# Converted weights are stored some pulls of the background queue later, and the words of the conversion lie in PSUM during the expert stage

## The chip, the core and the metric

The kernel runs on one core of a Trainium2 chip: TensorE (PE) with its weight loads (PEld), VectorE (DVE), ScalarE (ACT), GpSimd (POOL) and SyncE (SP), which issues nearly all DMA transfers. The metric is the device time of one execution in microseconds (us), as the median of several runs.

## What is computed

Three layers follow one another on 3072 tokens of width 384. The second is a top-1 mixture of 8 experts, and the third a gated product of two projections.

```python
# 1. gated linear attention (per batch and head)
state = f * state + k (outer) v ;  y = q @ state
# 2. mixture of experts: each token goes to one of 8 experts
h = maximum(x[mask] @ w1[e], 0);  out[mask] = gate * (h @ w2[e])
# 3. a, b = x @ w1, x @ w2;  out = ((a * b) @ w3) @ w_out
```

The weights of the third layer (w1, w2, w3, w_out of `moe2`) come as 64-bit floats. The kernel turns them into 32-bit floats by integer and scaling operations on the two 32-bit words of each number.

## The kernel before

The work is in three stages: attention with routing (to about 177 us of the profiled execution), the expert stage (about 177 to 424 us), and the gated layer (to the end). The order of instructions on each engine is written out by hand; engines run independently and wait for each other by semaphores.

**Expert stage.** Experts are taken one after another, `for e in range(E)`, with a window of 448 down to 376 tokens each. Each expert has eight steps `s`, one per 128 hidden units. In a step PE computes `hb` (`g1_step`, nine matmuls), then `acc` of the step before (`g2_step(e, s - 1)`, nine matmuls), so hidden units are used one step after they are made. Between the two, ACT makes `h[0] = relu(hb)` (L1030) and DVE the remainder `h[1]` (L1031); `acc` reads both. After step 7 the next expert's tokens are transposed (`xb`, L1015).

**Weights of the experts.** They are fetched by SP in halves of 768 KB into two buffers `stg` (L317): after step 3 and after step 7 the half of w1 (128x3x512), after steps 4 and 0 the half of w2 (128x4x384). ACT casts each piece (`wh`, L142) and POOL makes the remainder (`wl`, L143); these run piece by piece from a queue, `wsplit`, after each step. At step 0 SP also stores token numbers (`idd`, L995) and fetches the next expert's tokens (`xs`, L987, 675.5 KB). The gate factors are multiplied into `xs` by ACT in steps 3 to 6 (L1006).

**The background queue.** `bg` is a queue of Python generators that convert the third layer's weights; `bg.pull(n)` advances it by n places (3 per step, 4 in one expert). A piece of 128x512 numbers is converted in six pulls by `conversions`. SP loads it (`raw`, 512 KB, three buffers, L208). ACT makes the scaled low and high words (L224, L225, "the words" below). One pull later DVE shifts and masks (L227, L228). One pull later POOL adds (L230) into the tile `gt`. For the twelve pieces of w1 and w2, `to_scratch` then stores `gt` (256 KB) to a scratch tensor in device memory, `gd` (L149, "the store"). `gt` has two buffers, so the words of a piece reuse the tile of the piece two before it, and ACT waits at L224 until that tile's store has landed. The remaining eight pieces, of w3 (tile `g3`), are used in place by PE (`w3_turn`, `w3_times`).

The words of a piece stand at an odd step (1, 3, 5 or 7), behind that step's `h`; so one piece takes two steps. The loop puts the SP work of a step after its pulls:

```python
issue()
bg.pull(4 if e == E - 3 else 3)
wsplit.pull(...)
if s % 4 == 3:
    ahead = prefetch(2 * e + s // 4 + 2)
if s % 4 in (0, 3):
    step(ahead)
```

Matmul results of the expert stage lie in PSUM, in two sets of banks: three for `acc`, and five that `hb`, `xb` and the w3 tiles take in turn by `bank`. A class `Early` converts other pieces in the attention stage; there the scaled high word already lies in PSUM (`z`, L267; its bit operations are L272 and L273).

Of the kernel before, what the change touches and what calls it, by code (L numbers as in the profile page):

```python
# [10 lines left out]
I32 = mybir.dt.int32  # L11
AF = mybir.ActivationFunctionType
ALU = mybir.AluOpType
# [6 lines left out]
def attn_moe_glu_kernel(  # L20
# [17 lines left out]
    PE, V, A, G, SP = nc.tensor, nc.vector, nc.scalar, nc.gpsimd, nc.sync  # L38
# [3 lines left out]
    P = 128  # L42
# [18 lines left out]
    def bank(shape, name, tag="ps"):  # L61
        acc = tag == "acc"
        return psum[acc].tile(shape, F32, tag="acc" if acc else "ps", name=name)
# [49 lines left out]
    def f32(t):  # L113
        return t.bitcast(F32)
# [6 lines left out]
    class Background:  # L121
        def __init__(self):
            self.q = []

        def add(self, gen):
            self.q.append(gen)

        def pull(self, n):
            while n > 0 and self.q:
                try:  # L130
                    next(self.q[0])
                    n -= 1
                except StopIteration:
                    self.q.pop(0)

        def drain(self):
            while self.q:
                issue()
                self.pull(1)

    def split(src, hi, lo, eng=G):
        A.copy(out=hi, in_=src)  # L142
        eng.tensor_tensor(out=lo, in0=src, in1=f32(hi), op=ALU.subtract)  # L143

    def to_scratch(dst):
        def put(t):
            yield
            yield
            SP.dma_start(out=dst, in_=t)  # L149

        return put

# [41 lines left out]
    def issue():  # L194
        while loads:
            loads.pop(0)()

    def conversions(pieces):
        raws = {}

        def load_raw(i):
            if i < len(pieces):
                loads.append(lambda: fetch_raw(i))

        def fetch_raw(i):
            src, n, _, _ = pieces[i]
            raws[i] = cv.tile([P, 512, 2], I32, name="raw", bufs=RAW)[:, 0:n, :]
            SP.dma_start(out=raws[i], in_=src.bitcast(I32).rearrange("p (n w) -> p n w", w=2))  # L208

        for i in range(RAW):  # L210
            load_raw(i)
        for i, (_, n, tag, put) in enumerate(pieces):
            while i not in raws:
                yield
            if i == 0:
                for _ in range(8):
                    yield
            raw = raws.pop(i)
            lo, hi = raw[:, :, 0], raw[:, :, 1]
            z = lo  # L220
            pool, bufs = (cvw[1], cvw[2]) if tag == "g3" else (cv, 2)
            t = pool.tile([P, 512], F32, name=tag, bufs=bufs)[:, 0:n]
            p = t.bitcast(I32)
            A.activation(out=p, in_=lo.bitcast(U32), func=AF.Copy, scale=2.0 ** -29)  # L224
            A.activation(out=f32(z), in_=f32(hi), func=AF.Copy, scale=2.0 ** -112)  # L225
            yield
            V.tensor_scalar(out=z, in0=z, scalar1=3, scalar2=None, op0=ALU.logical_shift_left)  # L227
            V.scalar_tensor_tensor(out=z, in0=hi, scalar=-(1 << 31), in1=z, op0=ALU.bitwise_and, op1=ALU.bitwise_or)  # L228
            yield
            G.tensor_tensor(out=p, in0=z, in1=p, op=ALU.add)  # L230
            load_raw(i + RAW)
            yield
            yield
            yield from put(t)
# [58 lines left out]
    def late():  # L293
        pieces = []
        for n, g in enumerate((g1, g2)):
            for kk in range(KD):
                for c in range(FF // 512):
                    r, cs = slice(kk * P, (kk + 1) * P), slice(c * 512, (c + 1) * 512)
                    pieces.append((g[r, cs], 512, "gt", to_scratch(gd[n][r, cs])))
        return conversions(pieces + [w3_piece(i, c) for i in range(GAP_TILES, KF) for c in range(2)])  # L300
# [508 lines left out]
    with tc.manual_schedule():  # L809
# [57 lines left out]
        bg = Background()  # L867
# [379 lines left out]
        for n in range(NS):  # L1247
            end = n == NS - 1
            o1 = [bank2(1 - n % 2, DM, "ob") for _ in range(NT)]
            for s in range(KF):  # L1250
# [5 lines left out]
                if n == 0 and s == 3:  # L1256
                    t = stage[0].tile([P, KD, 512], F32R, tag="stg", name="stg")
# [164 lines left out]
```

## Time and profile before

| | us |
|---|---|
| median of 3 runs | 717.91 (717.73 to 719.16) |
| the profiled execution, its own time | 718.84 |
| its span, first to last instruction | 717.1 |
| PE busy | 698.7 (97%) |
| DVE busy | 454.4 (63%) |
| ACT busy | 364.1 (51%) |
| POOL busy | 345.1 (48%) |

The profiled execution is one run, taken by the hardware profiler; about 1.7 us of its time lie outside the span. Rows of a view give start, duration, engine, line of the kernel, operation, tiles as output<-inputs, and in square brackets the idle time just before with what ended it.

### The profile page before, as it was taken

To read this page: it belongs to the slowest core of one execution; us is meant where nothing else is said; L and a number is where in the kernel's file an instruction comes from. 1 tells how busy PE (TensorE), PEld (TensorE's weight loads), DVE (VectorE), ACT (ScalarE), POOL (GpSimd) and SP (SyncE) were. 2 spreads that over 40 slices of the span, in tenths; PEclk is the share of its full clock that TensorE was granted. 3 is DMA by queue.
4 is the path that set the end of the run, shared out by engine and by line. 5 is a ranking of instruction groups with operands and counts; after the bars stand their busy time and mean duration, and the time that the engine had idled before them with its cause. 6 is when DMAs were issued, how large, how long until landed. Compare 5 with 4: busy or idle time off the path is not lost.

```text
span 717.1 us, 13516 instructions
## 1 busy us (share of the span) xinstructions
PE 698.7 (97%) x5098; PEld 641.6 (89%) x5098; DVE 454.4 (63%) x860; ACT 364.1 (51%) x757; POOL 345.1 (48%) x420
## 2 busy tenths in 40 slices
PE   7999999999999999999999999999999999999995
PEld 6999989879999899999999998888988889888895
DVE  8989999987354554444465878854844457554461
ACT  5697877855656485555465544322522225321240
POOL 5466787784976677564660013222242222522233
PEclk9999999999999999999999999999999999999999
DMA  8999999852867758656342431000110001100002
GB/s 177 204 221 202 233 240 226 213 178 73 268 209 247 225 182 255 198 161 192 118 125 94 132 99 33 1 0 1 45 44 1 1 1 41 48 1 0 1 12 81
DMA packets 132033, 85.74 MB, mean 120 GB/s; under 512 B 106481, under 2 KB 114681, under 8 KB 131961
## 3 DMA queue, kind: packets, MB, share of 16 engines
q1 hardware_dynamic: 128489, 74.55, 38.9%
q0 software_dynamic: 3072, 9.46, 3.5%
q8 instruction: 42, 0.69, 0.4%
q10 hardware_dynamic: 400, 0.79, 0.4%
q14 instruction: 30, 0.25, 0.1%
HBM read 70.57 MB, written 14.22 MB: 118 GB/s over the span
## 4 chain that ended last, share of the span: by engine, by line
PE 63%; DMA 5%; POOL 2%; issue 2%; ACT 2%; SPq 1%; DVE 1%; POOLq 0%; DVEq 0%; ACTq 0%
PE ob L1231 14%; PE acc L1042 10%; PE hb L1028 9%; PE pd L1195 7%; PE pb L1195 7%; PE pa L1195 7%; PE pc L1195 5%; DMA stg<-in_moe_w_dram 4%; PE wpb L185 3%; POOL wl L143 1%; DMA gd<-gt 1%; PE xb L1015 1%; ACT wh L142 1%; POOL gt L230 1%; PE w3b L174 0%
## 5 line engine op out<-in xcount | busy, mean ns | idle before, releaser
L1198 POOL TENSOR_TENSOR xT<-xT,xT 128x512 f32<-128x512 f32 x48 | 63.9, 1332 | 194.0 <-ACT xT L1205 192.2
L143 POOL TENSOR_TENSOR wl<-stg,wh 128x384 fp32r<-128x384 f32 (+1 forms) x86 | 98.9, 1181 | 34.6 <-ACT wh L142 34.5
L1042 PE MATMUL acc<-h,wh 128*128 128x448 f32 (+7 forms) x384 | 105.4, 352 | 1.8 <-DVE h L1031 1.1
L1028 PE MATMUL hb<-xT,wh 128*128 128x448 f32 (+7 forms) x384 | 102.2, 347 | 0.0
L1031 DVE SCALAR_TENSOR_TENSOR h<-hb,h 128x448 fp32r<-128x448 f32 (+7 forms) x64 | 37.0, 578 | 86.5 <-ACT h L1030 86.3
L1220 ACT CAST abh<-xT 128x512 fp32r<-128x512 f32 x24 | 14.9, 621 | 133.7 <-DVE xT L1198 133.7
L1198 DVE TENSOR_TENSOR xT<-xT,pb 128x512 f32<-128x512 f32 x24 | 16.5, 688 | 97.8 <-PE pb L1195 91.4
L1042 PEld LDWEIGHTS acc<-h,wh 128*128 128x128 f32 x384 | 70.3, 188 | 6.4 <-DVE h L1031 3.6
L142 ACT CAST wh<-stg 128x384 fp32r<-128x384 f32 (+1 forms) x121 | 61.2, 562 | 25.8 <-DMA stg<-in_moe_w_dram 25.8
L1028 PEld LDWEIGHTS hb<-xT,wh 128*128 128x128 f32 x384 | 70.9, 188 | 1.2
L1028 PE MATMUL hb<-xT,wl 128*128 128x448 f32 (+7 forms) x192 | 66.6, 347 | 0.0
L1042 PE MATMUL acc<-h,wl 128*128 128x448 f32 (+7 forms) x192 | 66.6, 347 | 0.0
L1030 ACT ACTIVATE h<-hb 128x448 fp32r<-128x448 f32 (+7 forms) x64 | 32.4, 507 | 58.3 <-PE hb L1028 58.2
L1231 PE MATMUL ob<-wp,abh 128*128 128x384 f32 x240 | 61.8, 338 | 0.0
L1238 POOL DMA_INDIRECT out_dram<-h,didx x24 | 24.8, 1033 | 54.1 <-ACT h L1237 35.2
L1231 PEld LDWEIGHTS ob<-wp,abh 128*128 128x128 f32 x240 | 44.0, 188 | 1.8
L552 POOL TENSOR_SCALAR_AFFINE_SELECT am<-am 128x512 f32<-128x512 f32 x48 | 29.5, 640 | 25.8 <-ACT am L551 25.8
L1231 PE MATMUL ob<-wp,abl 128*128 128x384 f32 x120 | 40.5, 338 | 0.0
L185 PE MATMUL wpb<-wo,w3t 128*128 128x384 f32 x192 | 37.1, 341 | 0.0
L1198 DVE TENSOR_TENSOR xT<-xT,pc 128x512 f32<-128x512 f32 x48 | 33.0, 687 | 5.8 <-PE pc L1195 5.6
L1028 PEld LDWEIGHTS hb<-xT,wl 128*128 128x128 f32 x192 | 36.1, 188 | 0.6
L1042 PEld LDWEIGHTS acc<-h,wl 128*128 128x128 f32 x192 | 36.1, 188 | 0.6
(356 smaller groups left out, 1777.6 us busy)
## 6 DMA issues: line engine op xcount, KB each, us to landing
stg<-in_moe_w_dram SPq DMA_DIRECT2D x30, 768.0 KB
raw<-in_moe_w_dram SPq DMA_DIRECT2D x28, 512.0 KB
xs<-xsd SPq DMA_DIRECT2D x8, 675.5 KB
q<-in_q_dram SPq DMA_DIRECT2D x24, 192.0 KB
k<-in_k_dram SPq DMA_DIRECT2D x24, 192.0 KB
v<-in_v_dram SPq DMA_DIRECT2D x24, 192.0 KB
f<-in_f_logit_dram SPq DMA_DIRECT2D x23, 192.0 KB
raw<-in_moe_w_out_dram SPq DMA_DIRECT2D x8, 384.0 KB
```

The costliest lines, as they stand in the source:

```text
L142: A.copy(out=hi, in_=src)
L143: eng.tensor_tensor(out=lo, in0=src, in1=f32(hi), op=ALU.subtract)
L185: PE.matmul(out=o, lhsT=t[:, x, j, :], rhs=wo[:, y, j, :], start=(j + n == 0), stop=(j == KF - 1 and n == 2))
L552: G.affine_select(out=m[:, hb], in_=m[:, hb], pattern=[[0, NP], [1, P]], compare_op=ALU.is_ge, fill=0.0, base=0, channel_multiplier=-1)
L1028: PE.matmul(out=b, lhsT=w[x][:, kk, cs], rhs=xT[e][y][:, kk, :], start=(kk + n == 0), stop=(kk == KD - 1 and n == 2))
L1030: A.activation(out=h[0], in_=b, func=AF.Relu)
L1031: V.scalar_tensor_tensor(out=h[1], in0=b, scalar=0.0, in1=f32(h[0]), op0=ALU.max, op1=ALU.subtract)
L1042: PE.matmul(out=acc[d], lhsT=w[x][:, s % 4, d * P:(d + 1) * P], rhs=hs[s][y], start=(s + n == 0), stop=(s == KF - 1 and n == 2))
L1195: PE.matmul(out=o, lhsT=w[a][i][:, cs], rhs=x[b][j], start=(first and m == 0), stop=(last and m == 2), skip_group_check=True)
L1198: eng.tensor_tensor(out=out, in0=a, in1=b, op=op)
L1231: PE.matmul(out=o[t], lhsT=ab[x][:, t * P:(t + 1) * P], rhs=wp[:, y, s, :], start=(s + m == 0), stop=(s == KF - 1 and m == 2), skip_group_ ...
L1238: ins = G.indirect_dma_start(out=out, out_offset=bass.IndirectOffsetOnAxis(ap=didx[:, j:j + 1], axis=0), in_=r, in_offset=None,)
```

## The change

Two things are changed. First, `to_scratch` no longer issues the store at once. It puts it on a list, `late`, with a count of 4. `Background.tick` runs after every pull, the one of the entry too, and issues the store when its count is 0: three pulls, one step, later. Second, in `conversions` the scaled high word `z` goes to a PSUM bank of the five, in place of the `lo` half of `raw` in SBUF. DVE then takes both of its inputs' bits from `z` (the sign too, which it took from `hi` before) and writes into `lo`.

```diff
     class Background:
         def __init__(self):
             self.q = []
+            self.late = []
...
                     next(self.q[0])
                     n -= 1
+                    self.tick()
                 except StopIteration:
                     self.q.pop(0)
+
+        def tick(self):
+
+            for x in list(self.late):
+                x[0] -= 1
+                if x[0] == 0:
+                    self.late.remove(x)
+                    x[1]()
 
         def drain(self):
             while self.q:
                 issue()
                 self.pull(1)
+            while self.late:
+                self.tick()
...
             yield
             yield
-            SP.dma_start(out=dst, in_=t)
+            bg.late.append([4, lambda: SP.dma_start(out=dst, in_=t)])
...
             lo, hi = raw[:, :, 0], raw[:, :, 1]
-            z = lo
+            z = bank([P, 512], "z")[:, 0:n]
...
             A.activation(out=p, in_=lo.bitcast(U32), func=AF.Copy, scale=2.0 ** -29)
-            A.activation(out=f32(z), in_=f32(hi), func=AF.Copy, scale=2.0 ** -112)
-            yield
-            V.tensor_scalar(out=z, in0=z, scalar1=3, scalar2=None, op0=ALU.logical_shift_left)
-            V.scalar_tensor_tensor(out=z, in0=hi, scalar=-(1 << 31), in1=z, op0=ALU.bitwise_and, op1=ALU.bitwise_or)
-            yield
-            G.tensor_tensor(out=p, in0=z, in1=p, op=ALU.add)
+            A.activation(out=z, in_=f32(hi), func=AF.Copy, scale=2.0 ** -112)
+            yield
+            z = z.bitcast(I32)
+            V.tensor_scalar(out=lo, in0=z, scalar1=3, scalar2=None, op0=ALU.logical_shift_left)
+            V.scalar_tensor_tensor(out=lo, in0=z, scalar=-(1 << 31), in1=lo, op0=ALU.bitwise_and, op1=ALU.bitwise_or)
+            yield
+            G.tensor_tensor(out=p, in0=lo, in1=p, op=ALU.add)
```

The instructions on PE and POOL stand as before, and so do those of ACT and DVE but for the tiles named. On SP six of the twelve stores keep their place in the row, since nothing else stands in the step that they were put off by; the other six move. The first place is SP at the change of expert, here from expert 0 to 1. Before, from the store on (`TENSOR_LOAD` and `ISA` compute an address, `REGISTER_ALU` too):

```order
L149 DMA gd_86<-gt 128x512
L330 TENSOR_LOAD slot_e
L330 ISA x2
L317 ISA
L317 DMA stg<-in_moe_w_dram 128x3x512
L994 TENSOR_LOAD offs
L994 ISA x2
L995 REGISTER_ALU
L995 DMA idd<-xid 112x4
L985 TENSOR_LOAD slot_r
L985 ISA x2
```

And with the change, from the fetch of w1 on (the kernel's lines are 13 higher behind the edit):

```order
L330 DMA stg<-in_moe_w_dram 128x3x512
L1007 TENSOR_LOAD offs
L1007 ISA x2
L1008 REGISTER_ALU
L1008 DMA idd<-xid 112x4
L998 TENSOR_LOAD slot_r
L998 ISA x2
L1000 ISA
L1000 DMA xs<-xsd 112x1544
L161 DMA gd_86<-gt 128x512
L343 TENSOR_LOAD slot_e
L343 ISA x2
```

The store that stood ahead of the fetch of w1 now stands behind that fetch, the store of token numbers and the fetch of tokens, and ahead of the fetch of w2, whose address is computed in the last two rows.

The second place is SP in the middle of an expert (here expert 1). Before:

```order
L208 DMA raw<-in_moe_w_dram 128x1024
L149 DMA gd_86<-gt 128x512
L330 TENSOR_LOAD slot_e
L330 ISA x2
L317 ISA
L317 DMA stg<-in_moe_w_dram 128x3x512
L330 TENSOR_LOAD slot_e
L330 ISA x2
L317 ISA
L317 DMA stg<-in_moe_w_dram 128x4x384
```

And with the change:

```order
L220 DMA raw<-in_moe_w_dram 128x1024
L343 TENSOR_LOAD slot_e
L343 ISA x2
L330 ISA
L330 DMA stg<-in_moe_w_dram 128x3x512
L161 DMA gd_86<-gt 128x512
L343 TENSOR_LOAD slot_e
L343 ISA x2
L330 ISA
L330 DMA stg<-in_moe_w_dram 128x4x384
```

There the store moved behind the fetch of w1, between the two fetches. Each of the two places occurs three times.

The third place is ACT at the beginning of expert 2, steps 0 to 3, with the change; before it reads the same, but that the second row of the words writes `raw`.

```order
L1043 ACTIVATE h_3976<-hb 128x416
L1043 ACTIVATE h_4028<-hb 128x416
L236 ACTIVATE gt<-raw 128x512
L237 ACTIVATE z<-raw 128x512
L154 CAST wh<-stg 128x512 x3
L1043 ACTIVATE h_4066<-hb 128x416
L154 CAST wh<-stg 128x384 x2
```

Nothing moved here: the words (third and fourth row) stand ahead of the casts of w1's half and of the `h` of step 2, and the first of them takes the tile `gt` whose store moved at the change of expert.

## Rows read from the trace of the kernel before

**Rows 1.** Busy time by engine, expert stage: PE, PEld, DVE, ACT, POOL, clock, DMA
```profile
177.00:424.00 247.00, 244.21 (x1365) 235.66 (x1364) 134.22 (x212) 144.85 (x292) 133.42 (x112) 1.00 0.57 178
```

**Rows 2.** ACT in order of time, beginning of expert 2
```profile
241.89 0.66 ACT L224 ACTIVATE gt<-raw 128x512 int32<-128x512 uint32 x1
242.58 0.68 ACT L225 ACTIVATE raw<-raw 128x512 f32<-128x512 f32 x1
246.74 1.66 ACT L142 CAST wh<-stg 128x512 fp32r<-128x512 f32 x3 [3.48 <-DMA stg<-in_moe_w_dram]
248.31 0.51 ACT L1030 ACTIVATE h<-hb 128x416 fp32r<-128x416 f32 x1
251.23 0.93 ACT L142 CAST wh<-stg 128x384 fp32r<-128x384 f32 x2 [2.41 <-DMA stg<-in_moe_w_dram]
...
253.24 0.68 ACT L224 ACTIVATE gt<-raw 128x512 int32<-128x512 uint32 x1 [0.16 <-DMA gd<-gt]
```

**Rows 3.** PE in order of time: two stretches of experts 1 and 2
```profile
235.60 0.36 PE L1042 MATMUL acc<-h,wh 128*128 128x428 f32 x1
236.14 0.47 PE L1042 MATMUL acc<-h,wh 128*128 128x428 f32 x1 [0.18 <-DVE h L1031]
...
248.87 0.45 PE L1042 MATMUL acc<-h,wh 128*128 128x416 f32 x1 [0.48 <-ACT h L1030]
...
252.26 0.54 PE L1028 MATMUL hb<-xT,wh 128*128 128x416 f32 x2
...
252.83 0.88 PE L1042 MATMUL acc<-h,wh 128*128 128x416 f32 x2
```

**Rows 4.** SP's queue in order of time, change from expert 1 to 2
```profile
237.42 0.43 SPq L149 DMA_DIRECT2D gd<-gt  x1
...
241.32 0.35 SPq L987 DMA_DIRECT2D xs<-xsd  x1
242.50 0.40 SPq L317 DMA_DIRECT2D stg<-in_moe_w_dram  x1
...
243.83 0.53 SPq L149 DMA_DIRECT2D gd<-gt  x1
```

**Rows 5.** DMA issues of the page: KB of one issue
```profile
stg<-in_moe_w_dram SPq DMA_DIRECT2D x30, 768.0 KB
raw<-in_moe_w_dram SPq DMA_DIRECT2D x28, 512.0 KB
...
gd<-gt SPq DMA_DIRECT2D x12, 256.0 KB
```

**Rows 6.** ACT in order of time, beginnings of experts 1 and 3
```profile
217.26 0.52 ACT L1030 ACTIVATE h<-hb 128x428 fp32r<-128x428 f32 x1
220.16 0.93 ACT L142 CAST wh<-stg 128x384 fp32r<-128x384 f32 x2 [2.38 <-DMA stg<-in_moe_w_dram]
...
278.12 0.50 ACT L1030 ACTIVATE h<-hb 128x404 fp32r<-128x404 f32 x1
281.14 0.93 ACT L142 CAST wh<-stg 128x384 fp32r<-128x384 f32 x2 [2.52 <-DMA stg<-in_moe_w_dram]
```

**Rows 7.** ACT in order of time, middle of expert 1
```profile
230.34 1.66 ACT L142 CAST wh<-stg 128x512 fp32r<-128x512 f32 x3 [2.05 <-DMA stg<-in_moe_w_dram]
231.90 0.52 ACT L1030 ACTIVATE h<-hb 128x428 fp32r<-128x428 f32 x1
```

**Rows 8.** Groups by line and shape, DVE: busy us, mean ns
```profile
L228 DVE SCALAR_TENSOR_TENSOR raw<-raw 128x512 int32<-128x512 int32 x20 | 23.0, 1152 | 0.7
...
L273 DVE SCALAR_TENSOR_TENSOR raw<-z,raw 128x512 int32<-128x512 int32 x8 | 5.6, 694 | 0.3
```

**Rows 9.** PE in order of time, expert 5
```profile
347.84 0.66 PE L174 MATMUL w3b<-ident,g 128*128 128x128 f32 x4 [0.72 <-POOL g L230]
```

**Rows 10.** Busy time by engine at the end; columns as in group 1
```profile
709.00:710.00 1.00, 0.59 (x4) 0.26 (x2) 0.32 (x1) 0.00 (x0) 0.47 (x2) 1.00 0.17 55
...
714.00:715.00 1.00, 0.00 (x0) 0.00 (x0) 0.00 (x0) 0.00 (x0) 0.00 (x0) 0.73 0.04 8
```

## The prediction

> **What bounds the kernel now.** I read the busy time of the engines by stretch first. In the expert stage, the only one the change touches, PE is busy for 244.21 of 247 us at the full granted clock [rows 1]. So PE sets the time there: at most about 2.8 us of idle PE can be won, and any new wait of PE counts in full. The 64 steps take 247 / 64 = 3.9 us each on average. Next I read ACT in order of time, because PE's remaining gaps end on `h`, and `h` stands on ACT behind whatever ACT waits for. At the beginning of expert 2 ACT finishes a piece's words at 242.58 + 0.68 = 243.26, then idles 3.48 us until the w1 half has landed, casts it, and only then makes `h` of step 2 at 248.31 [rows 2]. PE has run dry by then: its `acc` starts at 248.87 after 0.48 us idle [rows 3]. When w2's half lands (251.23) there is a smaller stall: a pair of matmuls takes 0.88 us in place of 0.54 [rows 2, 3]. So at the change of expert what ends last is a DMA landing, ahead of `h` on ACT. The order of DMA transfers on SP's queue therefore decides, and that order is what the change edits. SP's queue I read third, for the times of issue [rows 4].
>
> **The moved stores, at the change of expert (three places).** Transfers land in the order of issue: the store issued at 243.83, behind w2's half and a raw load, is what ACT waits for at 253.24, 9.4 us later, though it is only 256 KB [rows 2, 4, 5]. Today the store at 237.42 is ahead of w1's half, so the tile is free when ACT comes to the next words of that tile at 241.89: no idle stands in that row. With the change this store is issued behind the token fetch (241.32) and ahead of w2's half (242.50) [rows 4], some 0.5 us before ACT already wants its tile, and with w1's half and the tokens ahead of it in the queue.
>
> When does it land? Behind w2's half (251.23) follow a raw load and a store, 768 KB, landed by 253.24 at the latest: 2.01 us, or 382 KB/us [rows 2, 5]. W2's half is also 768 KB, so what is directly ahead of it lands about 251.23 - 2.01 = 249.22. The set of bytes ahead of w2's half stays the same, so w2 itself doesn't move. ACT then has to do the words (243.26 - 241.89 = 1.37) and the three casts up to `h` (248.31 - 246.74 = 1.57): `h` starts at 249.22 + 1.37 + 1.57 = 252.16, which is 3.85 us later than now. PE waits for exactly this `h` and has nothing else in its row. The same sum at expert 1: 220.16 - 2.01 + 2.94 - 217.26 = 3.83; at expert 3: 281.14 - 2.01 + 2.94 - 278.12 = 3.95 [rows 6]. Together **+11.6**. DVE and POOL get their work behind this `h`, and SP's next raw load waits for POOL, so the whole pipeline shifts with PE and the delay isn't given back later.
>
> The bounds: the store can't land before w1's half, behind which it is queued. That half would itself land 256 / 382 = 0.67 us earlier, so the store's own 0.67 ends at 246.74 at the earliest, `h` at 249.68, +1.37 each, +4.1 in all. At the latest it lands with w2's half, 251.23: +5.86 each, +17.6. The value I take goes by the nearest measured rate.
>
> Given back: w2's casts find their data landed, so the stall at 252.83 goes (0.88 - 0.54 = 0.34); three like it, **-1.0** [rows 3].
>
> **The moved stores, in the middle of an expert (three places).** There the store moves behind w1's half only. Its landing is then where w1's landing is now, 230.34, and `h` follows at 230.34 + 2.94 = 233.28 in place of 231.90: +1.38 [rows 7]. The token scaling that the next transposes wait for stands right behind `h`, so PE feels it. In exchange the stall at 236.14 goes, where a matmul comes 0.54 us after its forerunner; the usual pace is 0.54 - 0.36 = 0.18 (the length of a pair less that of one), so 0.36 is saved [rows 3]. That is 1.38 - 0.36 = +1.02. It counts in experts 1 and 2. The third such place (expert 3) has no successor in `gt`: the later pieces use `g3`. So **+2.0**.
>
> **Six stores that don't move past anything:** nothing; SP runs ahead of the steps and isn't held by them.
>
> **Words in PSUM.** ACT's writes: same count, same length to a few hundredths. On DVE the mask-and-or drops from 1152 ns on average, stretched, to the 694 ns that the same form with PSUM input takes in the attention stage; over 20 pieces 20 x 0.46 = 9 us of DVE [rows 8]. DVE isn't the bound, so this shows only where PE waits for a sum behind it: the 0.72 us at 347.84 for POOL's sum of a w3 piece [rows 9]. With the 0.67 by which w1's half lands earlier in expert 3 the gain lies between 0 and 1.4; I take **-1.0**. The bank: `z` takes a turn among five. It is free again when DVE has done its two operations (about 2 x 0.7 us) in the following step, and in the instruction row PE comes to that bank a step or more later, 3.9 us; I cost it at 0. Were that cover gone, it would be up to 1.4 us for each of 20 pieces.
>
> **The sum:** 11.6 - 1.0 + 2.0 - 1.0 = +11.6. The rows come from an execution of 718.84 us with a span of 717.1; the median of the runs is 717.91. The shift is the same for both, so on the median it gives 717.91 + 11.6 = **729.5 us**.
>
> **Rivals.**
> *The clock falls in the longer gaps.* PE would idle 0.48 + 3.85 = 4.3 us at each change of expert. At the end of the kernel PE stops at 709.59, and the row of 714 to 715 has a mean clock of 0.73, so it fell to 0.5 (1.2 GHz) at 714.46: 4.87 us of idle at full clock first [rows 10]. That speaks for the clock holding, but with little to spare. No row shows how long it would stay down; if as long as it took to fall, half of 4.87 is lost, 2.4 us at each of one to three gaps: 732 to 737. The Trainium skill ("TensorE: Matmul & The Clock Gate", Part 1: The HAM clock gate) says the gate watches a free-running window, so the same idle can close it in one place and not in another; by that, this rival is a matter of chance at each gap, and one gap closing is likelier than three.
> *A shorter wait.* The store lands soon after w1's half, at the lower bound: 717.91 + 4.1 - 1.0 + 2.0 - 1.0 = 722.0, up to 726 for values between. For it: the tokens and the store might share the engines more evenly than my rate says. Against: the 9.4 us of the store at 243.83.
> *Faster.* The store's data overtakes the loads in the queue and lands about as fast as without them, before ACT wants the tile. Then the moves only help: w1's half lands 0.67 earlier at three changes of expert and w2's stays, so 717.91 - 3 x 0.67 - 1.0 = 714.9. It decides at a landing before 244.7: the words (1.37 us) are then done when w1's half lands, at 246.74 - 0.67. Against it stands again the 9.4 us, and ACT's 0.16 us on it [rows 2]. The Trainium skill ("DMA: Bandwidth & Descriptors", Queues, rings and completion order) says that an engine takes descriptors in ring order, though a later one may finish its write before an earlier one. By its first half the store queues, as in the trace; its second half is all that this rival has.
> *PSUM turns cost PE.* A `z` not yet read by DVE holds up a transpose or an `hb`: up to 1.4 us at some of 20 pieces. It would add to the forecast, not replace it, and is held within the range.
> *No effect.* The waits fall where ACT idles anyway (3.48 us at 243.26). It would need a landing near 244.7 with nothing won by w1's earlier landing.
>
> **The numbers.** My forecast, each change of expert costing 3 to 5 us at full clock, has 0.62 (727 to 733). The clock rival has 0.22, the shorter wait 0.10, faster 0.03, no effect 0.03. The range 724 to 736 leaves out faster, no effect, the lower end of the shorter wait and three falls of the clock, together about 0.17. A measurement of this kernel can tell about 0.2% (1.4 us) from no change. Slower by more than that has 0.62 + 0.22 + 0.10 = 0.94, the same 0.03, faster 0.03.
>
> **What would show it.** In the trace after: at the beginnings of experts 1, 2 and 3 ACT idles before the words, released by the DMA gd<-gt, for 6 to 8 us; the casts of w1 follow without idle; PE has three gaps of 4 to 5 us before `acc`, released by ACT's `h`; two gaps of 1 to 1.5 us in the transposes of experts 1 and 2; DVE's mask-and-or is 0.69 us everywhere; w2's casts wait less than 1 us at these places. I am wrong if the words at step 1 start without a wait for gd, if PE's gaps there stay under 1 us, or if PE waits for DVE's bit operations.

## The result, and the profile after

| | before | with the change |
|---|---|---|
| median, 6 runs each on one chip (us) | 718.31 (717.73 to 720.59) | 726.82 (725.96 to 727.45) |
| span of the profiled execution (us) | 717.1 | 725.1 |
| mean granted clock of the span | 0.998 | 0.992 |

The ratio is 1.0122, with a 95% interval of 1.0107 to 1.0137: slower by 8.5 us, and well above what can be told from no change. The forecast was 729.5 us, +11.6. So the sign was right, and the sum was 3 us too high. The measured 8.5 us also hold some 2 us that the lower clock cost and that were not in the sum; without them the sum was some 5 us too high.

Where the time went is read first from the first `hb` of each expert on PE, in the two profiled executions, one of each kernel. Expert 1 begins at 207.36 before and 207.34 after; it takes 31.31 us in place of 30.44, expert 2 takes 34.26 in place of 30.61, expert 3 takes 33.96 in place of 30.51. That is +0.87, +3.65 and +3.45, together 8.0; behind expert 3 the shift stays the same to the end. The forecast by these places was +4.5, +4.5 and +3.6, less 1.0 for the words in PSUM (a part of it in expert 3, a part in expert 5).

The busy time by stretch of the kernel after: the whole expert stage (it answers to [rows 1]), then two stretches with the beginnings of experts 2 and 3, then two short ones within them. Columns as in [rows 1].

```profile
177.00:432.00 255.00, 246.10 (x1365) 238.98 (x1364) 125.93 (x213) 141.45 (x292) 129.49 (x112) 0.99 0.55 172
243.00:278.00 35.00, 31.35 (x163) 30.17 (x162) 14.58 (x25) 17.93 (x37) 21.12 (x19) 0.95 0.65 206
278.00:309.00 31.00, 27.51 (x150) 26.75 (x149) 11.68 (x21) 17.30 (x36) 19.93 (x18) 0.94 0.63 211
...
253.00:257.00 4.00, 3.83 (x12) 3.52 (x12) 3.31 (x5) 3.35 (x8) 4.00 (x4) 0.57 0.02 4
287.00:291.00 4.00, 4.00 (x13) 3.94 (x14) 1.80 (x4) 3.01 (x7) 4.00 (x5) 0.57 0.01 2
```

PE is idle for 8.9 us of the stage in place of 2.8, and the clock is no longer 1.0: in two stretches of 4 us its mean is 0.57, that is (1 - 0.57) / 0.5 x 4 = 3.4 us at the lower level (1.2 GHz) in each.

ACT in order of time after, at the beginnings of experts 1, 2 and 3 and in the middle of expert 1 (answers to [rows 2], [rows 6] and [rows 7]):

```profile
214.91 0.66 ACT L236 ACTIVATE gt<-raw 128x512 int32<-128x512 uint32 x1 [3.29 <-DMA gd<-gt]
...
230.54 0.67 ACT L236 ACTIVATE gt<-raw 128x512 int32<-128x512 uint32 x1 [3.64 <-DMA gd<-gt]
...
249.51 0.66 ACT L236 ACTIVATE gt<-raw 128x512 int32<-128x512 uint32 x1 [6.61 <-DMA gd<-gt]
250.07 0.61 ACT L237 ACTIVATE z<-raw 128x512 f32<-128x512 f32 x1
250.61 1.64 ACT L154 CAST wh<-stg 128x512 fp32r<-128x512 f32 x3
252.16 0.51 ACT L1043 ACTIVATE h<-hb 128x416 fp32r<-128x416 f32 x1
...
283.18 0.66 ACT L236 ACTIVATE gt<-raw 128x512 int32<-128x512 uint32 x1 [6.18 <-DMA gd<-gt]
```

The mechanism is the forecast one: ACT waits for the store of its tile, the casts of w1 follow without idle, and `h` of expert 2 starts at 252.16, the very time that was worked out. That the hundredths agree is luck: the wait ends at 249.51, not 249.22, and the words take 1.10 us (249.51 to 250.61), not 1.37. At expert 1 the wait is half as long. What it does to PE (answers to [rows 3]):

```profile
218.13 0.46 PE L1055 MATMUL acc<-h,wh 128*128 128x428 f32 x1 [0.18 <-ACT h L1043]
...
234.29 1.02 PE L1028 MATMUL xb<-ident,xs 104*128 104x104 f32 x9 [1.13 <-ACT xs L1019]
...
248.89 0.34 PE L1041 MATMUL hb<-xT,wl 128*128 128x416 f32 x1
252.72 0.45 PE L1055 MATMUL acc<-h,wh 128*128 128x416 f32 x1 [3.48 <-ACT h L1043]
253.34 0.72 PE L1055 MATMUL acc<-h,wh 128*128 128x416 f32 x1 [0.17 <-DVE h L1044]
...
254.20 0.90 PE L1055 MATMUL acc<-h,wh 128*128 128x416 f32 x2
...
286.38 0.45 PE L1055 MATMUL acc<-h,wh 128*128 128x404 f32 x1 [3.33 <-ACT h L1043]
```

There are two gaps of 3.3 to 3.5 us, not three of 4 to 5, and one of 1.13 in the transposes of expert 1, not two. At 254.20 a pair of matmuls takes 0.90 in place of 0.55: the lower clock. SP's queue at the beginnings of experts 1 and 2 (answers to [rows 4]) shows why expert 1 got off lightly:

```profile
203.92 0.34 SPq L220 DMA_DIRECT2D raw<-in_moe_w_dram  x1
205.09 0.40 SPq L330 DMA_DIRECT2D stg<-in_moe_w_dram  x1
...
207.46 0.35 SPq L1000 DMA_DIRECT2D xs<-xsd  x1
207.85 0.43 SPq L161 DMA_DIRECT2D gd<-gt  x1
...
237.41 0.33 SPq L220 DMA_DIRECT2D raw<-in_moe_w_dram  x1
238.60 0.39 SPq L330 DMA_DIRECT2D stg<-in_moe_w_dram  x1
...
241.31 0.43 SPq L161 DMA_DIRECT2D gd<-gt  x1
```

The raw load that stands ahead of w1's fetch goes out 3.42 us before expert 1 begins (207.34 - 203.92) and 1.24 us before expert 2 does (238.65 - 237.41). I call this SP's lead. DVE's groups by line and shape (answer to [rows 8]) give the likely reason, which the experiments below test:

```profile
L241 DVE SCALAR_TENSOR_TENSOR raw<-z,raw 128x512 int32<-128x512 int32 x20 | 13.8, 692 | 0.7
L240 DVE TENSOR_SCALAR raw<-z 128x512 int32<-128x512 int32 x20 | 13.7, 684 | 4.3 <-ACT z L237 3.8 <-issue 0.5
```

### The profile page after: what moved, and what is told of

It reads as the page before. It is cut to its first block, busy times and chain, and to the rows that moved or that the text cites. A ratio compares the mean times of both kernels' runs of the same rounds, so it can differ in the third digit from the quotient of the medians.

```text
span 725.1 us, 13516 instructions
## 1 busy us (share of the span) xinstructions
PE 700.8 (97%) x5098; PEld 644.7 (89%) x5098; DVE 444.8 (61%) x860; ACT 360.5 (50%) x757; POOL 341.0 (47%) x420
## 4 chain that ended last, share of the span: by engine, by line
PE 79%; DMA 6%; DVE 5%; issue 3%; ACT 3%; POOL 2%; SPq 1%; POOLq 0%; ACTq 0%; DVEq 0%
PE ob L1244 14%; PE acc L1055 11%; PE hb L1041 9%; PE pd L1208 7%; PE pb L1208 7%; PE pa L1208 7%; PE pc L1208 5%; DMA gd<-gt 4%; PE wpb L197 3%; PE a L558 3%; PE y L593 2%; PE xl L640 2%; PE y L585 2%; PE qt L509 1%; DMA f<-in_f_logit_dram 1%
## 5 line engine op out<-in xcount | busy, mean ns | idle before, releaser
L155 POOL TENSOR_TENSOR wl<-stg,wh 128x384 fp32r<-128x384 f32 (+1 forms) x86 | 95.3, 1138 | 48.6 <-ACT wh L154 48.6
```

## The experiments

All ratios are to the kernel before, run on the same chip in turn with the experiment. Three chips were used, and before has a median of 715.1 to 716.7 us on them, so ratios are compared, not times.

**The two halves apart.** Stores where they were, words in PSUM:

```diff
-            bg.late.append([4, lambda: SP.dma_start(out=dst, in_=t)])
+            bg.late.append([1, lambda: SP.dma_start(out=dst, in_=t)])
```

> The store's count is 1 in place of 4, so all twelve stores stand on SP where they stood before; only the words' place in PSUM is changed. Theory (the loss is ACT's wait for the moved store, and PSUM words help): no wait of ACT for gd of more than 0.2 us, clock 1.0 throughout, 715.5 to 717.8 us, faster than before by 0.5 to 2.5 us, since DVE's bit operations no longer stretch and SP's raw load and the w1 fetch behind it go out up to 2 us earlier. Rival (the loss comes from z taking turns among the PSUM banks): 722 us or more, with PE waiting for DVE's bit operations.

Measured: 0.9951 (0.9936 to 0.9966), 711.25 us. This half is a gain of 3.5 us, three times the 1.0 of the forecast. It is also more than the 0.5 to 2.5 us expected of this run. ACT waits half as long for the halves of w1 and w2 (`wh` for the DMA stg). ACT's waits in the kernel before, then in this one (total us, times, longest):

```profile
ACT wh L142 <- DMA stg<-in_moe_w_dram: 25.8, 13, 3.5
```

```profile
ACT wh L154 <- DMA stg<-in_moe_w_dram: 13.1, 8, 3.4
```

And the other half, late stores with the words in SBUF as before (against the kernel before; `tick` as in the change):

```diff
-            SP.dma_start(out=dst, in_=t)
+            bg.late.append([4, lambda: SP.dma_start(out=dst, in_=t)])
```

> The store's count is 4, the words lie in SBUF as before. Theory (in the changed kernel, expert 1 lost only 0.9 us because the shorter bit operations let SP issue expert 1's fetches about 2 us earlier): expert 1 now loses 3 to 5 us like experts 2 and 3, three falls of the clock or two, 728 to 731 us. Rival (PSUM words do nothing for the time, and expert 1 was cheap because its fetch happened to land faster): 726 to 727.5 us, expert 1 again under 1.5 us.

Measured: 1.0235 (1.0218 to 1.0251), 731.19 us, 16 us slower. The two halves add up to +1.9% (1.0235 and 0.9951), the change has +1.2%: the words in PSUM take off more beside late stores (1.1%) than alone (0.5%). PE's step from the last `hb` to `acc` is 3.8 to 3.9 us here at all three changes of expert; expert 1 isn't spared. The clock fell in all three, in the third for longer:

```profile
210.00:243.00 33.00, 29.24 (x146) 27.08 (x145) 14.95 (x21) 17.49 (x36) 19.95 (x17) 0.95 0.59 194
243.00:278.00 35.00, 30.39 (x155) 28.62 (x154) 16.97 (x23) 18.45 (x37) 20.51 (x19) 0.95 0.62 195
278.00:309.00 31.00, 27.49 (x140) 26.69 (x139) 13.26 (x20) 16.50 (x33) 19.26 (x17) 0.89 0.63 210
```

**Does the late store cost through its tile alone?** The change, with pieces taking tiles of `gt` and `g3` in pairs by turns, so four tiles in place of two:

```diff
+            tag = "g3" if i % 4 > 1 else tag
```

> The changed kernel, but the pieces take turns among four tiles, two of gt and two of g3, so the tile that the words take had its store two pieces earlier. Theory (the loss is ACT's wait for the store in a reused tile): ACT's waits for gd are gone (under 0.5 us in all), clock 1.0, 714.5 to 717.5 us, since w1's half is no longer behind the store. Rival (the new order of transfers on the queue itself costs, by landing w1's or w2's half later): 721 us or more with ACT waiting for stg.

Measured: 0.9953 (0.9938 to 0.9967), the same as with the stores in place. The waits of ACT for `gd` are gone and PE has no gap left at the changes of expert:

```profile
243.00:309.00 66.00, 66.00 (x376) 65.64 (x375) 30.25 (x52) 40.27 (x84) 44.95 (x40) 1.00 0.64 209
```

So nothing but the wait for the reused tile costs; the order of the transfers, by itself, costs nothing that these runs can tell. The same with the words in SBUF (against the kernel before; `tick` as in the change):

```diff
-            SP.dma_start(out=dst, in_=t)
+            bg.late.append([4, lambda: SP.dma_start(out=dst, in_=t)])
...
             z = lo
+            tag = "g3" if i % 4 > 1 else tag
```

> Words in SBUF as in the kernel before, every store four pulls on, and two more tiles for the pieces (gt and g3 by turns in pairs), so that no words wait for a store. My theory: the late store costs through its tile alone, and behind it w1's half lands up to 0.67 us earlier at three changes of expert: 0.996 to 1.000, with ACT's waits for gd gone and the clock at 1.0. Rival, that the order of the queue itself costs (w2's half or the tokens come later): above 1.004.

Measured: 1.0013 (0.9998 to 1.0028): 1.0235 falls nearly to 1, though not below it as expected. One wait is left in its trace, in expert 3, where pieces of w3 are `g3` too and the words take a tile whose store landed only at 288.74. ACT, and behind it PE:

```profile
288.81 0.66 ACT L237 ACTIVATE g<-raw 128x512 int32<-128x512 uint32 x1 [3.88 <-issue]
```

```profile
292.67 0.98 PE L1028 MATMUL xb<-ident,xs 99*128 99x99 f32 x9 [1.93 <-ACT xs L1019]
```

The profile names no releaser for the first row, and the store's landing 0.07 us before it is the nearest event. PE's 1.93 us, and a clock of 0.94 behind it (278 to 309 us), are more than the 0.13% that the run is above 1.

**What the clock costs.** The change, with 24 small matmuls of no use put into PE's row at step 3 of experts 1, 2 and 3, where it would idle:

```diff
+                if s == 3 and 1 <= e <= 3:
+                    warm(24)
```

> The changed kernel with 24 matmuls of 128x128 added on PE in each of the three gaps (step 3 of experts 1, 2 and 3, ahead of acc), about 1.4 us of work whose result nobody reads. Theory (two falls of the clock of 3.4 us each cost up to 1.7 us each): the clock stays at 1.0 in the expert stage, ACT's waits for gd are as long as without them, and the time falls to 723.4 to 725.5 us. Rival (the falls cost nothing, as PE only catches up with ACT): 726 to 727.5 us; a second rival (the clock falls nevertheless): the same, with the clock under 1.0 in experts 2 and 3.

Measured: 1.0095 (1.0077 to 1.0113), clock 1.0 through the stage, though ACT still waits 18.3 us for `gd`. The difference to 1.0122 is 0.27%, 1.9 us, for two falls; the intervals touch, so the size is rough. The rows give somewhat more: in 3.4 us at half clock PE does the work of 1.7, and experts 2 and 3 take 32.80 and 32.84 us here, 1.46 and 1.12 less than in the change. Expert 1, which had no long gap to fill, takes 0.44 more (31.75).

```profile
243.00:278.00 35.00, 32.82 (x195) 31.66 (x194) 13.99 (x23) 17.93 (x37) 20.50 (x18) 1.00 0.66 218
278.00:309.00 31.00, 28.93 (x181) 27.80 (x180) 12.81 (x23) 18.00 (x37) 19.11 (x17) 1.00 0.66 215
```

**The places apart.** Words in PSUM, and only the stores in the middle of an expert late (`at[0]` holds the step):

```diff
+            bg.late.append([4 if at[0] == 3 else 1, lambda: SP.dma_start(out=dst, in_=t)])
```

> Words in PSUM; a store that is appended at step 3 goes out four pulls on (the three places in the middle of an expert), every other store goes out where it did before. My theory: only the middle of experts 1 and 2 gets a wait for the tile, about 1 us each, so +1 to +2 us over the run with the words in PSUM alone (0.9951): a ratio of 0.996 to 0.999, the clock at 1.0 through the expert stage, and no long idle before h at a change of expert. Rival, that all six moved stores cost alike (some 2.6 us each by the distance from that run to the changed kernel): three of them give 1.004 to 1.007.

Measured: 0.9968 (0.9952 to 0.9985). In its trace no wait of PE in the expert stage is over 0.3 us, experts 1 and 2 take as long as with the words in PSUM alone (29.11 and 28.55 us), and only expert 3 takes longer, by 0.48. So the wait of about 1 us each that was expected in experts 1 and 2 isn't there. And only those at a change of expert (`at[0] == 7`):

> Words in PSUM; a store that is appended at step 7 goes out four pulls on (the three changes of expert), every other store where it did before. My theory: these three carry nearly all of the loss, so a ratio of 1.004 to 1.011 by whether the clock falls in the gaps, with ACT idle for 5 to 7 us before the words at experts 2 and 3 and PE idle for about 3.5 us behind it. Rival, that all six moved stores cost alike: 1.003 or less, with PE gaps of about 2 us.

Measured: 1.0054 (1.0036 to 1.0072). From 0.9951 the first is +0.2% (1.2 us, within the intervals' reach of nothing), the second +1.0% (7.4 us): the places aren't alike. ACT's waits, of 5.12 and 2.94 us at experts 2 and 3, and PE's gap of 2.00 us at expert 2 are shorter than expected. Both together make +1.7% in the change, 0.5% (3.7 us, from four ratios, so rough) more than the sum. The traces show where it comes from. By SP's lead: with the stores late only at the changes of expert, SP's lead is 2.88, 1.97 and 3.21 us before experts 1, 2 and 3, where the change has 3.42, 1.24 and 1.07; with the stores late only in the middle it is 3.04, 2.55 and 1.79, and with none late 3.58, 3.67 and 3.21. With the stores late only at the changes, ACT's long wait is the one at expert 2, PE's gap behind it is 2.00 us, and behind the shorter wait at expert 3 PE has no gap over 0.3 us (two rows of ACT, then one of PE):

```profile
246.38 0.66 ACT L237 ACTIVATE gt<-raw 128x512 int32<-128x512 uint32 x1 [5.12 <-DMA gd<-gt]
...
276.73 0.67 ACT L237 ACTIVATE gt<-raw 128x512 int32<-128x512 uint32 x1 [2.94 <-DMA gd<-gt]
...
249.60 0.46 PE L1056 MATMUL acc<-h,wh 128*128 128x416 f32 x1 [2.00 <-ACT h L1044]
```

So late stores in the middle of expert 1 or 2 go with a shorter lead at the next change. The likely way is that a wait there delays the next pieces, and with them the raw load that stands in SP's queue ahead of the next w1. The middle then costs little where it stands, and more at the next change of expert if the store there is late too. One fall of the clock more, two in the change and one here, is in the 3.7 us as well.

**Why do the words in PSUM gain?** Stores in place, words in PSUM, DVE's two operations on each piece done twice:

```diff
-            V.tensor_scalar(out=lo, in0=z, scalar1=3, scalar2=None, op0=ALU.logical_shift_left)
-            V.scalar_tensor_tensor(out=lo, in0=z, scalar=-(1 << 31), in1=lo, op0=ALU.bitwise_and, op1=ALU.bitwise_or)
+            for _ in range(2):
+                V.tensor_scalar(out=lo, in0=z, scalar1=3, scalar2=None, op0=ALU.logical_shift_left)
+                V.scalar_tensor_tensor(out=lo, in0=z, scalar=-(1 << 31), in1=lo, op0=ALU.bitwise_and, op1=ALU.bitwise_or)
```

> Words in PSUM, every store where it was before, and VectorE's two bit operations on each piece done twice over with the same result: about 1.4 us more of VectorE for each of the expert stage's pieces, and no other engine has more to do. My theory of why the words in PSUM alone gained 0.5%: the length of the bit operations sets when POOL's sum ends, and with it when the next raw piece and the w1 half behind it in SP's queue go out. Then the gain is gone: 0.999 to 1.003, raw loads about as late as in the kernel before. Rival, that the gain lies with ACT or POOL, whose operations no longer share operands with VectorE's: VectorE's length doesn't matter, the ratio stays at 0.997 or less.

Measured: 1.0006 (0.9991 to 1.0021). The gain is gone. The chain ahead of expert 2 is, in the kernel before (all engines in order of time, the rows of DVE, POOL and SP for one piece):

```profile
232.46 0.60 DVE L1031 SCALAR_TENSOR_TENSOR h<-hb,h 128x428 fp32r<-128x428 f32 x1 [4.65 <-ACT h L1030]
232.98 0.90 DVE L227 TENSOR_SCALAR raw<-raw 128x512 int32<-128x512 int32 x1
233.91 1.67 DVE L228 SCALAR_TENSOR_TENSOR raw<-raw 128x512 int32<-128x512 int32 x1
...
235.71 1.31 POOL L230 TENSOR_TENSOR gt<-raw,gt 128x512 int32<-128x512 int32 x1 [0.68 <-POOL wl L143]
237.04 0.33 SPq L208 DMA_DIRECT2D raw<-in_moe_w_dram  x1
...
238.69 0.39 SPq L317 DMA_DIRECT2D stg<-in_moe_w_dram  x1
```

and with the words in PSUM alone:

```profile
226.86 0.60 DVE L1044 SCALAR_TENSOR_TENSOR h<-hb,h 128x428 fp32r<-128x428 f32 x1 [2.97 <-ACT h L1043]
...
228.10 0.69 DVE L241 SCALAR_TENSOR_TENSOR raw<-z,raw 128x512 int32<-128x512 int32 x1
229.20 1.31 POOL L243 TENSOR_TENSOR gt<-raw,gt 128x512 int32<-128x512 int32 x1
...
230.54 0.33 SPq L220 DMA_DIRECT2D raw<-in_moe_w_dram  x1
```

POOL's sum needs DVE's second result; in the kernel before it starts 0.13 us behind it (235.58 to 235.71), though its row names POOL's `wl`, which had ended 0.68 us earlier. SP's raw load waits for the sum (it reuses the buffer that the sum read), and w1's fetch stands behind the raw load. From `h` on DVE to the raw load it is 4.58 us before and 3.68 with the words in PSUM; done twice it is 4.87 at the same place (229.56 to 234.43). SP's lead before expert 2 is 0.76, 3.67 and 1.43 us in the three: more than these 0.9 us apart. The likely reason is that a w1 half that lands earlier no longer holds up the casts and `h`, and so the next piece; no run tests this by itself.

The doubling costs by a second way too. In its trace PE waits for `h` of DVE itself, behind the longer bit operations, up to 0.53 us at a time. Expert 5, which comes after the last store, takes 33.81 us in place of 32.86 with the words in PSUM alone and 32.91 before:

```profile
339.19 0.45 PE L1056 MATMUL acc<-h,wh 128*128 128x388 f32 x1 [0.53 <-DVE h L1045]
```

Experts 1 to 3 together take 88.75 us, between 86.15 (words alone) and 91.56 (before). So the run shows that the length of DVE's operations matters; in its trace about half of what experts 1 to 3 had won is lost again, and how much of the gain goes through SP's raw load alone stays open.

The same doubling in the changed kernel tests whether this lead also sets the price of the late store:

> The changed kernel (stores four pulls on, words in PSUM), with VectorE's two bit operations on each piece done twice over with the same result. My theory: the late store's wait is set by how long before an expert's first hb SP issues the raw load that stands ahead of w1's fetch (3.4 us before expert 1 in the changed kernel, where the gap of PE is short, and 1.1 to 1.2 us before experts 2 and 3, where it is 3.5 us). Longer bit operations take that lead away, so expert 1 too gets a PE gap of about 3.5 us and perhaps a clock fall: some 3 to 6 us more than the changed kernel, 1.016 to 1.023, near the late stores with words in SBUF (1.0235). Rival, that the words in PSUM help through ACT or otherwise than by this lead: VectorE's length does not matter, 1.010 to 1.014, and expert 1 stays short.

Measured: 1.0231 (1.0209 to 1.0253), as with late stores and words in SBUF, and at the upper end of what was expected. Expert 1 takes 35.33 us in place of 31.31. Its PE gap is shorter than expected (1.73 us); there is a second one of 1.95 us in the transposes, and a lower clock behind that (mean 0.92 from 222 to 243 us):

```profile
217.78 0.46 PE L1056 MATMUL acc<-h,wh 128*128 128x428 f32 x1 [1.73 <-ACT h L1044]
```

Over the traces with late stores on SP and two tiles, PE's step from the last `hb` to `acc` at a change of expert goes by SP's lead (each number from one row of SP and two of PE). With a lead of 2.88 us or more the step is at most 0.54, with 1.97 or less at least 2.09; within the two groups the order doesn't hold:

| kernel, expert | SP's lead, us | PE's step, us |
|---|---|---|
| the change, 1 | 3.42 | 0.54 |
| late at changes only, 3 | 3.21 | 0.45 |
| late at changes only, 1 | 2.88 | 0.34 |
| late at changes only, 2 | 1.97 | 2.35 |
| change, DVE doubled, 1 | 1.74 | 2.09 |
| change, DVE doubled, 2 | 1.66 | 3.09 |
| the change, 2 | 1.24 | 3.83 |
| the change, 3 | 1.07 | 3.67 |
| change, DVE doubled, 3 | 0.69 | 4.44 |
| words in SBUF, 1 to 3 | 0.52 to 0.75 | 3.78 to 3.89 |

**Is it SP's queue?** The change, with these stores issued by ACT:

```diff
-            bg.late.append([4, lambda: SP.dma_start(out=dst, in_=t)])
+            bg.late.append([4, lambda: A.dma_start(out=dst, in_=t)])
```

> The changed kernel with the twelve stores of the expert stage issued from ScalarE in place of SP, at the same pull. My theory: the late store costs because it stands behind w1's half and the tokens in SP's queue; on another queue it lands within 3 to 4 us of its issue, ACT's wait for its tile falls under 1.5 us, no PE gap is over 1.5 us, the clock stays at 1.0: 0.995 to 1.002, with ScalarE busy some 0.4 us more per store. Rival, that the engines are full and serve the transfers by time of issue whichever queue they come from: the store lands no sooner than in the changed kernel, 1.009 or more.

Measured: 1.0107 (1.0085 to 1.0129); single runs lie between 718.1 and 724.8 us, and the profiled one is the fastest. My theory fell, though the rival, that the store lands no sooner, isn't quite what the trace shows either. ACT's waits for `gd` are still 15.2 us in four, and the store that ACT issues at 238.53 lands by 245.09, 6.6 us later, behind w1's half that SP issued at 236.25 (its last part landed at 243.17) and ahead of the tokens issued at 238.64 (246.71). In the change the store went out behind the tokens and ACT waited for it 8.2 us from its issue (241.31 to 249.51). The last row is PE's, at expert 3:

```profile
236.25 0.39 SPq L330 DMA_DIRECT2D stg<-in_moe_w_dram  x1
...
238.53 0.33 ACTq L161 DMA_DIRECT2D gd<-gt  x1
238.64 0.35 SPq L1000 DMA_DIRECT2D xs<-xsd  x1
...
245.09 0.66 ACT L236 ACTIVATE gt<-raw 128x512 int32<-128x512 uint32 x1 [4.33 <-DMA gd<-gt]
...
279.10 0.45 PE L1055 MATMUL acc<-h,wh 128*128 128x404 f32 x1 [2.03 <-ACT h L1043]
```

These transfers landed by the time of issue, whichever engine issued them. The Trainium skill ("DMA: Bandwidth & Descriptors", Issuing engines are not separate DMA queues) says that transfers from different engines run on the same 16 DMA engines, and that another issuer saves only the time of issue; the 6.6 us agree. In this trace the clock stays at 1.0 through the stage, even behind the gap of 2.03 us in the last row. Why the runs of this kernel spread so widely stays open, since only the fastest has a trace; the clock is a part of it, as its mean over a run is 0.997 in the fastest and 0.991 in the slowest.

## Why the prediction was right in sign and mechanism, and where its sum was off

- **What decides.** That the order of landings ahead of `h` decides, with ACT behind the reused tile, is shown: with four tiles the loss is gone. As for the place, two of the three changes of expert paid in the way that was forecast; at expert 1 PE's gap is 0.18 us, under the 1 us that the prediction named as a sign of being wrong. The bound of 2.8 us that PE's idle time set on any gain was wrong. The words in PSUM alone gain 3.5 us by the runs (2.4 to 4.6 by the interval), and in the traces, which are from two chips, experts 1 to 3 are shorter by 5.4 us (86.15 in place of 91.56). PE's rows also hide waits as slow matmuls: behind the 0.48 us of idle in [rows 3], `acc` comes in steps of 0.62 us (248.87 to 249.49) where the pace is 0.19.
- **The change of expert, +11.6.** The landing rate held: the wait at expert 2 ended at 249.51, where 249.22 was worked out. It held in absolute time because SP issued w1 within 0.1 us of the old time (238.60 and 238.69), though the expert itself began 0.85 us later. The term failed in a premise that went unsaid, that SP issues as long before the expert as in [rows 4]. The other half of the change moved that: at expert 1 SP's lead is 3.42 us in place of 1.46 (207.36 - 205.90 before), and the term is 0.3 us in place of 3.8 (PE's step, 0.22 to 0.54). Where the lead was short, at experts 2 and 3, PE's step grew by 3.0 us (0.83 to 3.83) and 3.2, not 3.85 and 3.95, since these experts also began later than before. Together that is 6.5 us in place of 11.6. The 1.0 given back is there: at experts 1 to 3 w2's casts stand behind `h` without a wait.
- **The middle of an expert, +2.0.** At expert 1 the gap is there (1.13 us in the transposes); at expert 2 none is left. By itself this part measured 1.2 us, within the noise, with no such gap in its trace; beside late stores at the changes it costs some 3.7 us more, by a shorter lead of SP and one fall of the clock more, which the forecast did not have.
- **Words in PSUM, -1.0.** In proportion this term was off the most: -3.5 us alone (-0.49% of 715). "DVE isn't the bound" was true and beside the point: DVE's operations stand in the chain DVE, POOL, SP's raw load, w1's fetch, ACT, `h`, and with shorter ones the raw load went out 0.9 us sooner behind `h`. Doubled, they take the gain back, in part by PE's own wait for DVE's `h`. ACT's part was also put too low: a pair of words takes 1.10 us (249.51 to 250.61) where [rows 2] has 1.37; with DVE doubled ACT's words are as short, so this alone doesn't hold the gain. On the 0.69 us of each operation the forecast was right (means of 692 and 684 ns). The stretch of the old form beside POOL, up to 1.67 us above, is as the Trainium skill ("SBUF — State Buffer", Who interferes with whom) has it: a VectorE operation with two inputs in SBUF contends with a GpSimd one that reads SBUF, one with at most one such input, outside the 2-port modes, doesn't. The trace agrees, 1152 and 692 ns; no run here shows the port itself.
- **PSUM turns and the six unmoved stores at 0.** Right: with four tiles and late stores, or with words alone, PE shows no wait for a bank and the kernel is at 0.995.
- **The clock.** The likeliest case had it at full speed, by 4.87 us of idle at the end of the kernel [rows 10]. It fell just behind both long gaps, of 3.5 and 3.3 us, as the rival said, at some 1.9 us for the two by the dummies' run, where the rival had 2.4 for each. So the rival happened, and the time stayed in the range of the main case because the other terms were smaller. Taking one idle time from one place as a bound was the mistake: with the stores late at changes only, it fell behind a gap of 2.0 us (mean 0.95 from 243 to 278 us), and with the stores on ACT it held through one of 2.03.

The 8.5 us measured, split by the runs: words in PSUM -3.5, late stores at the changes +7.4, in the middle +1.2, and the rest, some +3.5, from these two together. The clock's 1.9 is within these. That the total lies only 3 us from the forecast is in part luck: the changes of expert cost less than forecast and the words gained more, while the clock and the effect of the two places on each other, neither of them in the sum, added to it.

## What to carry to other kernels

In this kernel the edit that put a transfer off was priced by what was queued ahead of it when it went out and by who reused its buffer; two more tiles made the same edit free. An engine with idle time can still set the end, if its operations lead to the issue of a fetch: follow the chain from its output to the next issue in a DMA queue before calling its time hidden. Price two edits of one chain together: here the second took back half of what the first cost. The version with the words in PSUM and the stores in place is the fastest (711.25 us, 0.9951); the change with four tiles is level with it (711.55 us, 0.9953).

## What the hardware showed that I had not expected

- A mean clock of 0.57 in two stretches of 4 us: two falls of about 3.4 us, each just after PE had resumed from a gap of 3.3 to 3.5 us. A gap of 2.00 us was followed by such a fall too, while one of 2.03 us, with the stores on ACT, was not, and PE at the end of the kernel before stood idle for 4.87 us at full clock first. So in these runs the length of a gap alone doesn't tell. Gaps that were filled down to 1.04 and 1.46 us with small matmuls kept the clock at 1.0.
- A store of 256 KB that ACT issued on its own queue landed 6.6 us later, behind the 768 KB that SP had issued 2.3 us before it. Issued by another engine, it still didn't pass them.
